# Padding TensorE's program: the fetch times of the search and the grain of its places

## The chip, the cores and the metric

The kernel runs on one core of a Trainium2 chip. The metric is the device time of one execution in microseconds; lower is better. Three runs of the kernel before gave 807.34 (the median), 804.82 and 808.4 us.

## The reference

Two blocks with residuals. The first is a recurrent attention over 64 segments of 32 tokens: eight memory rows stand ahead of each segment's tokens, and the eight memory rows that come out of a segment go into the next, so the segments form a chain. The second block is a pre-norm MLP (512 to 1792 to 512, tanh-gelu) on the result.

```python
for s in range(n_seg):                                  # 64 segments of 32 tokens
    h = jnp.concatenate([mem, xs], axis=1)              # 8 memory rows + 32 tokens, 512 wide
    q = jnp.einsum('btd,dhe->bhte', h, Wq)              # 32 heads of 128; k and v alike
    scores = jnp.where(mask, einsum(q, k) * scale, -1e9)
    o = jnp.einsum('bhqk,bhke->bhqe', softmax(scores), v)
    o = jnp.einsum('bhte,hed->btd', o, Wo)
    mem = o[:, :M, :].copy()                            # into the next segment
    outs.append(o[:, M:, :])
h = x + A(layernorm(x));  h2 = h + B(layernorm(h))
```

## The kernel before

All operations are recorded first. A scheduler (class `Sched`, lines 136 to 660) then sets the order on each engine, wires the semaphores and emits the program. On TensorE the order of a segment is written out by hand (`ORDERS`, line 39), as a list of parts; on the other engines a table of due times (`PLAN`, line 45) sets it. The parts of a segment are, in TensorE's order:

- Q0 and K0, in turns, and then Q1 and K1: the projections of the memory rows' part of `h` (`hT`) with Wq and Wk, in units of four 128x512 matmuls (lines 686 and 943);
- V0, SC0, V1, SC1, V1: the projection with Wv, in two halves, and between its units the scores' correction by the mask and the memory (SC0 and SC1, line 1119, sixteen matmuls each that wait for `BD` and `ZC`, which GpSimd makes);
- F: four filler units of work that is not on the chain, for the token blocks ahead or behind (lines 686, 943 and 1300). Two stand ahead of PV0, one ahead of SA, one behind it;
- PV0, PVA, PV1: the products of probabilities and values (lines 1150, 1154, 1222 and 1228), which wait for the values `VS` that ScalarE casts;
- WO: eight units of the output projection, 64 matmuls of 128x256 (line 1261). VectorE turns their result into the next segment's `hT` (`TT`, line 1273; `hT`, line 1267);
- SA: scores of 32 matmuls (line 1176), which cover the time until that `hT` is there.

So a segment ends when WO has gone through VectorE, and Q0 of the next waits for it.

**Fetches of the program.** TensorE's instructions come in blocks of 256 (`FETCH_N`; 16 KB, one transfer on the queue that the profile calls q8 instruction). The scheduler chooses where in the stream a block begins. It can add weight loads that nothing uses ("pads", line 941) to the units of the projections. A unit has at most `PADS` of them and a block at most `PAD_MAX`, counted in steps of `PAD_STEP`. A dynamic program (`pads`, line 494) goes over all places at which a block can begin, and adds up a cost for each pair of successive beginnings:

```python
wait = LATE.get("F2" if part == "F" and behind else part, 1.0) + ...      # line 516
c = c0 + sum(w * max(0.0, f + FETCH_TOOK + FETCH_IN + m - took) for m, w in FAR) + 1e-4 * p   # line 542
g = round(max(late[b], f + FETCH_TOOK + FETCH_REST - took), 1)            # line 543
```

Here `took` is the planned time between the two beginnings. `f` is the time from the entry of a block until the fetch of the next one starts; it is taken from the table `LATE` by the unit in which the block begins ("F2" is an F behind PVA). `FETCH_TOOK` is how long a fetch lasts, and `FETCH_IN` the time from its landing to the first instruction that can be used. What is left over is a stall of TensorE. Below, a place "enters" a part when the first instruction of a block lies in it.

Two other steps read the result: `windows` (line 392) puts the DMAs of SyncE's queue into the time behind a fetch, and `pauses` (line 371) gives up to three units behind a block's beginning a wait on earlier work of TensorE itself.

Of the kernel before, what the change touches and what calls it, by code (L numbers as in the profile page):

```python
# [21 lines left out]
DMA_SEMS, SOFT_SEMS = 100, 8  # L22
SORT = True
FETCH_N, FETCH_US = 256, 0.0
FETCH_AT, PADS, PAD_MAX, PAD_STEP = 65, 8, 104, 8
FAR = ((-0.1, 1.0), (0.2, 0.6), (0.5, 0.2))
FETCH_TOOK, FETCH_REST, FETCH_IN, LAST = 1.2, 2.45, 1.1, 1.5
LATE = dict(Q0=0.1, K0=0.1, Q1=-0.5, K1=-0.4, V0=2.0, SC0=2.0, SC1=1.6, V1=1.8, F=1.3, PV0=1.0, PVA=1.0, PV1=0.95, WO=0.4, F2=0.5, SA=0.5)
KEEP = True
WINDOWS, WIN_LO, WIN_HI, WIN_BEHIND = True, 1.0, -0.8, 0.4  # L30
PAUSES, PAUSE_IN, PAUSE_US = 3, 64, 0.5
# [108 lines left out]
class Sched:  # L140
# [353 lines left out]
    def pads(self):  # L494
# [17 lines left out]
        for i in range(lo, hi):  # L512
            o, n = pe[i], where[i + 1] - where[i]
            part = "" if o.tag is None else o.tag[1]
            behind = part == "PVA" or behind and part not in ("Q0", "K0")
            wait = LATE.get("F2" if part == "F" and behind else part, 1.0) + LAST * (o.tag is None or o.tag[0] == NS - 1)
            for k in range(n):
# [133 lines left out]
F = 1792  # L651
# [1122 lines left out]
```

## Time and profile before

| | |
|---|---|
| median of 3 runs | 807.34 us |
| profiled execution | 809.47 us, span 807.7 us, TensorE's mean granted clock 0.992 |
| TensorE matmul busy | 771.6 us, 96% of the span |
| VectorE, ScalarE, GpSimd busy | 588.0, 530.4, 312.0 us |
| instruction fetches | 156 packets of 16 KB |

The profiled execution is one run, 2.13 us above the median of the three. Its span is 1.77 us shorter than its time; that rest lies around the program. Groups of instructions are named by line, engine, operation and tiles; "PEld" is the weight load and "PE" the matmul. A row of the timeline gives a start, the duration of a run of equal instructions, their number, and in brackets the idle time ahead of them with what ended it ("issue" is time in which the engine waited for nothing that the profile shows).

### The profile page before, as it was taken

What the parts mean: (1) busy time and instruction counts of PE and PEld (TensorE: products, weight loads), DVE (VectorE), ACT (ScalarE), POOL (GpSimd) and SP (SyncE); (2) the same over time, 40 slices, a digit from 0 to 9 for tenths busy, and PEclk for the clock granted to TensorE, in tenths of its full rate; (3) what the DMA queues carried; (4) which work ended last, traced back from release to release, by engine and by line L of the source; (5) the groups of instructions that cost most, each with busy time, mean ns of one, the idle gap of its engine ahead of it and who ended that gap; (6) DMA issues with size and microseconds to landing.
All of it is one profiled execution on the core that took longest, in us unless ns stands there. A gap on an engine that the chain in (4) does not pass through costs nothing.

```text
span 807.7 us, 44856 instructions
## 1 busy us (share of the span) xinstructions
PE 771.6 (96%) x19564; PEld 423.2 (52%) x20093; DVE 588.0 (73%) x1865; ACT 530.4 (66%) x1380; POOL 312.0 (39%) x836
## 2 busy tenths in 40 slices
PE   3688999999999999999999999999999999899998
PEld 1345455555555555555655555556655554444443
DVE  3267888888888888888888888888897888723211
ACT  2446777777677777777767777767777777733342
POOL 3013223444443434344434444434443434267200
PEclk9979999999999999999999999999999999999999
DMA  9960000111101010101010101020112221255200
GB/s 338 393 189 12 2 23 18 27 33 27 33 20 41 18 42 18 43 15 47 14 47 9 51 6 47 11 50 4 50 30 66 53 59 40 75 140 167 73 27 26
DMA packets 65453, 48.11 MB, mean 60 GB/s; under 512 B 29028, under 2 KB 61676, under 8 KB 65260
## 3 DMA queue, kind: packets, MB, share of 16 engines
q1 hardware_dynamic: 64928, 44.98, 19.6%
q8 instruction: 156, 2.56, 1.3%
q14 instruction: 37, 0.30, 0.1%
q10 hardware_dynamic: 332, 0.27, 0.1%
HBM read 31.08 MB, written 8.13 MB: 49 GB/s over the span
## 4 chain that ended last, share of the span: by engine, by line
PE 91%; DVE 3%; DMA 2%; SPq 2%; ACT 1%; issue 1%; POOL 0%; DVEq 0%; POOLq 0%
PE high L943 33%; PE high L686 17%; PE quad L1261 15%; PE quad L1663 6%; PE high L1656 5%; PE high L1300 3%; DMA WQ<-in_A_Wq_dram 2%; PE quad L1119 2%; SPq L846 2%; PE quad L1176 2%; PE quad L1222 2%; PE high L1455 1%; PE high L1150 1%; PE quad L1150 1%; PE high L1261 1%
## 5 line engine op out<-in xcount | busy, mean ns | idle before, releaser
L943 PE MATMUL high<-WQ,hT 128*32 128x512 bf16 x1796 | 157.8, 381 | 3.1 <-DVE hT L1267 2.7
L1199 POOL TENSOR_TENSOR PA<-SA,rsa 128x256 bf16<-128x256 f32 x64 | 39.6, 619 | 237.1 <-DVE rsa L1191 139.3
L686 PE MATMUL high<-WK,hT 128*32 128x512 bf16 x1260 | 127.6, 379 | 0.1
L1261 PE MATMUL quad<-WO,OT 128*32 128x256 bf16 x4032 | 122.4, 273 | 0.2 <-issue 0.2
L943 PE MATMUL high<-WV,hT 128*32 128x512 bf16 x1528 | 116.4, 380 | 0.0
L962 ACT ACTIVATE kq<-high 128x512 bf16<-128x512 f32 x160 | 94.2, 598 | 27.2 <-PE high L943 24.4
L961 ACT CAST kq<-high 128x512 bf16<-128x512 f32 x159 | 92.6, 582 | 22.0 <-PE high L943 20.5
L1261 PEld LDWEIGHTS quad<-WO,OT 128*32 128x32 bf16 x4032 | 102.3, 97 | 6.1 <-issue 1.4
L1207 POOL COPY BD<-PTA 32x128 f32<-32x128 f32 x256 | 79.9, 312 | 16.8 <-DVE PTA L1203 0.6
L943 PEld LDWEIGHTS high<-WQ,hT 128*32 128x32 bf16 x1796 | 52.0, 95 | 61.3 <-issue 27.2
L984 DVE STREAM_TRANSPOSE KALL<-kq 128x256 f32<-128x256 f32 x160 | 69.5, 435 | 12.0 <-ACT kq L961 9.1
L961 ACT CAST VS<-high 128x512 bf16<-128x512 f32 x126 | 73.1, 580 | 0.0
L941 PEld LDWEIGHTS <-hT 128*32 128x32 bf16 x3064 | 49.8, 96 | 33.4 <-DVE hT L1267 6.3
L1273 DVE STREAM_TRANSPOSE TT<-quad 128x256 f32<-128x256 f32 x63 | 28.3, 449 | 50.7 <-PE quad L1261 50.6
L1659 ACT ACTIVATE WQ<-high,b1t 128x512 bf16<-128x512 f32 x42 | 28.9, 687 | 51.9 <-PE high L1656 51.9
L961 ACT CAST OT<-quad 128x128 bf16<-128x128 f32 (+1 forms) x128 | 47.8, 375 | 21.8 <-PE quad L1154 21.5
L1018 ACT COPY KALL<-KALL 128x128 f32<-128x128 f32 x62 | 18.4, 297 | 59.0 <-PE quad L1176 58.8
L984 DVE STREAM_TRANSPOSE QT<-kq 128x256 f32<-128x256 f32 x128 | 54.9, 429 | 1.4 <-ACT kq L962 1.2
L943 PE MATMUL high<-WK,hT 128*32 128x512 bf16 x788 | 55.3, 379 | 0.0
L1119 PEld LDWEIGHTS quad<-KALL,ZC 128*32 128x32 bf16 x2016 | 32.3, 96 | 42.3 <-POOL BD L1207 18.4
L686 PE MATMUL high<-WV,hT 128*32 128x512 bf16 x520 | 53.8, 382 | 0.0
L1313 POOL TENSOR_TENSOR opT<-TTB,TTS 32x64 bf16<-32x64 f32 x128 | 40.1, 313 | 34.9 <-DVE opT L1267 18.3
(184 smaller groups left out, 1620.3 us busy)
## 6 DMA issues: line engine op xcount, KB each, us to landing
WV<-in_A_Wv_dram SPq DMA_DIRECT2D x4, 1024.0 KB, 10.2
WK<-in_A_Wk_dram SPq DMA_DIRECT2D x4, 1024.0 KB, 17.9
WQ<-in_A_Wq_dram SPq DMA_DIRECT2D x4, 1024.0 KB, 20.2
WO<-in_A_Wo_dram SPq DMA_DIRECT2D x16, 256.0 KB, 7.6
v_last<-VSB SPq DMA_DIRECT2D x60, 64.0 KB, 2.2
VBD<-v_last SPq DMA_DIRECT2D x60, 64.0 KB, 2.6
h_mid<-xr SPq DMA_DIRECT2D x16, 128.0 KB, 2.2
WQ<-h_mid SPq DMA_DIRECT2D x4, 512.0 KB, 4.3
```

What stands on the lines that cost most here:

```text
L686: return e.add_instruction(mybir.InstMatmult(name="I-%d" % (4000000 + _kept[0]), engine=mybir.EngineType.PE, start_tensor_calc=start, stop ...
L941: e.ldweights(l, tile_position=(0, 32 * j))
L943: ins = e.matmul(o, l, m, start=(k == 0), stop=(k == DC - 1), tile_position=(0, 32 * j), skip_group_check=True)
L961: return {"act": (lambda e: e.copy(out, src), t_act(n, ps_)), "dve": (lambda e: e.tensor_copy(out, src), 0.155 + 1.0e-3 * n * fast)}
L962: return {"act": (lambda e: e.mul(out, src, scale_), t_act(n, ps_)), "dve": (lambda e: e.tensor_scalar(out, src, scale_, None, ALU.mult), ...
L984: S.op("dve", lambda e: e.transpose(out, src), reads=[("kq", i)], writes=[key], dur=t_dve(256) + 0.02)
L1119: ins = e.matmul(o[32 * j:32 * j + 32, :], zc_window(h), rhs, start=False, stop=(i == 3), tile_position=(0, 32 * j), skip_group_check=True)
L1207: S.narrow(S.op("pool", lambda e, j=j, rows=rows: e.tensor_copy(words(BD[rows, par, :, j, :, :]), words(PTA[rows, 0:4])), reads=["PTA"], w ...
L1261: ins = e.matmul(ps[bank][32 * j:32 * j + 32, 0:256], lhs(slot(h)), wo_cols(h, b), start=(k == 0), stop=(k == 15), tile_position=(0, 32 * ...
L1313: return e.tensor_tensor(o[32 * q:32 * q + 32, c:c + 2], x, y, ALU.add)
L1656: ins = e.matmul(ps[bank][:, 0:SBT], W1[:, cc, fc * P:(fc + 1) * P], hnT_of(k)[:, cc, :], start=(cc == 0), stop=(cc == DC - 1))
L1663: S.op("pe", lambda e: e.matmul(quad[:, t, :], gT_of(k, fc)[:, t * P:(t + 1) * P], W2[:, fc, :], start=(fc == 0), stop=(fc == FC - 1)), re ...
```

## The change

Three lines of constants change; no function does.

```diff
 FETCH_N, FETCH_US = 256, 0.0
-FETCH_AT, PADS, PAD_MAX, PAD_STEP = 65, 8, 104, 8
+FETCH_AT, PADS, PAD_MAX, PAD_STEP = 65, 12, 144, 4
 FAR = ((-0.1, 1.0), (0.2, 0.6), (0.5, 0.2))
-FETCH_TOOK, FETCH_REST, FETCH_IN, LAST = 1.2, 2.45, 1.1, 1.5
-LATE = dict(Q0=0.1, K0=0.1, Q1=-0.5, K1=-0.4, V0=2.0, SC0=2.0, SC1=1.6, V1=1.8, F=1.3, PV0=1.0, PVA=1.0, PV1=0.95, WO=0.4, F2=0.5, SA=0.5)
+FETCH_TOOK, FETCH_REST, FETCH_IN, LAST = 1.2, 2.45, 1.38, 1.5
+LATE = dict(Q0=0.4, K0=0.6, Q1=0.0, K1=1.25, V0=2.0, SC0=2.0, SC1=1.6, V1=1.85, F=1.55, PV0=1.1, PVA=1.1, PV1=1.05, WO=0.7, F2=0.9, SA=0.9)
```

The streams of VectorE (1,709 rows), ScalarE (1,173) and GpSimd (501) are row for row those of before. On SyncE's queue a few issues (`v_last`, `h_mid`, `xT`) trade places. TensorE's matmuls keep their order. What moves is the pads: 3,224 before (403 units with 8 each) and 3,252 now (254 units with 12, 17 with 8, 17 with 4). The number of blocks stays 156, so what changes is where they begin. Over the segments 1 to 63 the beginnings fall into these parts:

| part entered | WO | K1 | F | SA | Q1 | Q0 | PV1 | K0 | SC1 | PVA | V0, PV0 |
|---|---|---|---|---|---|---|---|---|---|---|---|
| before | 24 | 26 | 24 | 19 | 14 | 13 | 13 | 8 | 0 | 4 | 2 |
| now | 30 | 22 | 14 | 7 | 16 | 16 | 15 | 7 | 14 | 3 | 3 |

**At the start of segment 27, on TensorE.** `WQ,hT` is a unit of Q0 or Q1, `WK,hT` one of K0. Before:

```order
L686 MATMUL high<-WK,hT 32x512 x4
L943 MATMUL high<-WQ,hT 32x512 x4
L686 MATMUL high<-WK,hT 32x512 x4
L686 MATMUL high<-WQ,hT 32x512 x4
L943 MATMUL high<-WQ,hT 32x512 x12
```

Now, from the same rows (three of the four matmuls of each unit, with their pads, left out):

```order
L686 MATMUL high<-WK,hT 32x512
L941 LDWEIGHTS hT x3
...
L686 MATMUL high<-WQ,hT 32x512
L941 LDWEIGHTS hT x3
L943 MATMUL high<-WQ,hT 32x512
...
L941 LDWEIGHTS hT
L943 MATMUL high<-WQ,hT 32x512
```

Three unused loads now stand ahead of each matmul there (12 in a unit, some units have 4), where there were none. The block that begins in Q0 of this segment ends, with them, in SC1; before, a block that began in Q1 ended in PV1.

**From SC1 to the last WO unit of segment 27, on TensorE**, where a block now begins inside the first row below and the next one inside the WO row. The rows are the same before and now:

```order
L1119 MATMUL quad<-KALL,ZC 32x64 x16
L943 MATMUL high<-WV,hT 32x512 x8
L1300 MATMUL high<-WO,OTB 32x512 x16
L1150 MATMUL quad<-PTC,VS 128x2x8 x8
L1154 MATMUL quad<-PTC,VBD 128x64 x2
L1222 MATMUL quad<-BD,VS 128x2x32 x16
L1228 MATMUL quad<-BDL,VBD 128x8x8 x4
L1150 MATMUL high<-PTC,VS 128x2x8 x8
L1154 MATMUL high<-PTC,VBD 128x64 x2
L1261 MATMUL quad<-WO,OT 32x256 x64
```

Nothing in this stretch can take a pad, so its length in time is fixed. From SC1 (one of its last three instructions of 33) to the twelfth of the sixteen instructions of WO's last unit it is one block in six segments (11, 19, 27, 35, 43 and 51). In eight others (6, 14, 22, 30, 38, 46, 54 and 57) the block that begins in SC1 ends in the F unit ahead of SA, just behind WO.

## The prediction

> **What bounds the kernel now.** I read the page first, for the busy shares and the chain that ended last.
>
> ```profile
> PE 771.6 (96%) x19564; PEld 423.2 (52%) x20093; DVE 588.0 (73%) x1865; ACT 530.4 (66%) x1380; POOL 312.0 (39%) x836
> q8 instruction: 156, 2.56, 1.3%
> PE 91%; DVE 3%; DMA 2%; SPq 2%; ACT 1%; issue 1%; POOL 0%; DVEq 0%; POOLq 0%
> ```
>
> TensorE is the bound, and its matmuls keep their order. So the change can only win or lose time in which TensorE has nothing to do, or is slowed. The second row gives a mean fetch: 1.3% of 16 engines over 807.7 us, by 156, is 1.08 us.
>
> Then I read the period of a segment from VectorE's transposition of WO's result, which comes once a segment. The first row is its group with the first and last start; the others are single ones of the timeline (start, duration).
>
> ```profile
> L1273 DVE STREAM_TRANSPOSE TT<-quad x63: 411/450/452, 61.7 to 698.2; 128x256 f32<-128x256 f32 x63
> ...
> 307.58 0.45 DVE L1273 STREAM_TRANSPOSE TT<-quad 128x256 f32<-128x256 f32 x1 [1.22 <-PE quad L1261]
> 317.71 0.45 DVE L1273 STREAM_TRANSPOSE TT<-quad 128x256 f32<-128x256 f32 x1 [0.41 <-PE quad L1261]
> ...
> 410.02 0.45 DVE L1273 STREAM_TRANSPOSE TT<-quad 128x256 f32<-128x256 f32 x1 [0.91 <-PE quad L1261]
> 420.60 0.45 DVE L1273 STREAM_TRANSPOSE TT<-quad 128x256 f32<-128x256 f32 x1 [0.51 <-PE quad L1261]
> 430.69 0.45 DVE L1273 STREAM_TRANSPOSE TT<-quad 128x256 f32<-128x256 f32 x1 [1.22 <-PE quad L1261]
> ...
> 667.17 0.45 DVE L1273 STREAM_TRANSPOSE TT<-quad 128x256 f32<-128x256 f32 x1 [0.50 <-PE quad L1261]
> 698.19 0.45 DVE L1273 STREAM_TRANSPOSE TT<-quad 128x256 f32<-128x256 f32 x1 [1.24 <-PE quad L1261]
> ```
>
> 636.5 us over 62 periods is 10.266 us a segment. The best take 10.09 (420.60 to 430.69), others 10.58 (410.02 to 420.60). 62 times the difference of 0.176 is **10.9 us: all that better places can win.** The last three periods take 31.02 us, 0.75 over 30.27, though few pads lie there; I put 1.7 us of the 10.9 (0.7 to 3) to other causes. That leaves 9.2 for fetches.
>
> What such a stall is shows in the weight loads ahead of SA, in segment 35 and, without a stall, in segment 25.
>
> ```profile
> 406.07 0.77 PEld L1300 LDWEIGHTS high<-WO,OTB 128*32 128x32 bf16 x16
> 407.26 0.17 PEld L1150 LDWEIGHTS quad<-PTC,VS 64*128 64x128 bf16 x8 [0.42 <-ACT VS L961]
> 410.79 0.28 PEld L1176 LDWEIGHTS quad<-KALL,QT 128*32 128x32 bf16 x32 [0.89 <-issue]
> ```
>
> ```profile
> 303.66 0.11 PEld L943 LDWEIGHTS high<-WQ,hB 128*32 128x32 bf16 x4
> 304.85 0.17 PEld L1150 LDWEIGHTS quad<-PTC,VS 64*128 64x128 bf16 x8 [0.64 <-ACT VS L961]
> 307.57 0.51 PEld L1176 LDWEIGHTS quad<-KALL,QT 128*32 128x32 bf16 x32 [0.22 <-issue]
> ```
>
> In both, one block begins in the F units (406.1, 303.66) and the next in SA (410.79 and 307.8, inside the row that starts at 307.57). The DMA view of short windows tells when the next block was fetched. For 406.1 to 407.95 it has no row of that queue; for 407.95 to 409.35 it has the first row below. For 303.7 to 305.5 it has no packet at all (second row), and for 305.5 to 306.5 the third.
>
> ```profile
> q8 instruction: 1, 0.02, 5.9%
> DMA packets 0, 0.00 MB, mean 0 GB/s; under 512 B 0, under 2 KB 0, under 8 KB 0
> q8 instruction: 1, 0.02, 5.7%
> ```
>
> 5.9% of 16 engines over 1.4 us is a fetch of 1.32 us, so it started within 0.08 us of 407.95 and landed at 409.3. SA's first load came 1.46 to 1.52 us later. In segment 25 it took 0.91 us, started 1.84 to 1.93 us after the entry, and landed at 306.5, 1.3 us before SA went on. So a stall is: wait from entry to the fetch's start (1.85 from F), the fetch (1.08), landing to use (1.3 to 1.5), less the time between the two places.
>
> **The change part by part.**
>
> *The pads themselves: 0.* A unit with 12 pads issues 16 loads, one with 8 issues 12. Windows of one unit of Q0 or K0 each, in a padded stretch (the second number in brackets is of weight loads):
>
> ```profile
> 309.21:309.42 0.21, 0.21 (x8) 0.15 (x12) 0.21 (x2) 0.21 (x2) 0.00 (x0) 1.00 0.00 0
> 309.42:309.64 0.22, 0.22 (x9) 0.13 (x9) 0.22 (x2) 0.22 (x1) 0.00 (x0) 1.00 0.00 0
> 309.64:309.86 0.22, 0.22 (x10) 0.16 (x13) 0.22 (x2) 0.22 (x2) 0.00 (x0) 1.00 0.00 0
> ```
>
> From 9 loads to 13 the loads' busy time goes from 0.13 to 0.16 us, 8 ns a load, and a unit stays at 0.22. Four more make 0.19, still below; the four matmuls of the unit hide them. Without that cover they would cost 0.03 us in each of 254 units, 7.6 us in all; I take 0. *SyncE's DMAs that trade places: 0.* Of the page's issues these are the two that recur each segment, one behind the other:
>
> ```profile
> v_last<-VSB SPq DMA_DIRECT2D x60, 64.0 KB, 2.2
> VBD<-v_last SPq DMA_DIRECT2D x60, 64.0 KB, 2.6
> ```
>
> They take 4.8 us of a period of 10.27, so about 5 us of slack hides a shift; if one came late, PV0 or PVA would wait for `VBD`, at most the shift of one fetch window, some 1 us in few segments.
>
> *The stalls that go.* By the table of places, F to SA comes 7 times instead of 18 or 19. The Q0 and K0 entries that followed 3.0 to 3.5 us behind the one before (about 21) now follow after 3.5 us or more but for two; PV1 entered from K1 (3) and the second F of a segment from its first (3) are gone. So some 46 short pairs carry the 9.2 us, 0.2 us each. The 7 that remain run from F's first unit to the eighth instruction of SA, a shape like segment 25's: 10.13 us from 307.58 to 317.71, 0.04 over the floor. I take 0.06 each, **0.4** (bounds 0 and 7 x 0.2 = 1.4). The two short Q0 and K0 pairs (3.2 and 3.3 us) keep 0.25 each, **0.5**. For fetches that happen to last 1.3 or 1.4 us where the pair has little to spare (WO, K1) I take **1.0** (0 to 2.0).
>
> *The stalls that come.* Fourteen blocks now begin in SC1, which none did before, and the table's 1.6 us for it is unchanged. Segment 27, loads:
>
> ```profile
> 323.56 0.21 PEld L1119 LDWEIGHTS quad<-KALL,ZC 128*32 128x32 bf16 x16 [0.31 <-POOL BD L1207]
> 323.69 0.14 PEld L943 LDWEIGHTS high<-WV,hT 128*32 128x32 bf16 x8
> ...
> 325.12 0.17 PEld L1150 LDWEIGHTS quad<-PTC,VS 64*128 64x128 bf16 x8 [0.42 <-ACT VS L961]
> ...
> 325.90 1.65 PEld L1261 LDWEIGHTS quad<-WO,OT 128*32 128x32 bf16 x64
> 327.55 0.22 PEld L1300 LDWEIGHTS high<-WO,OTB 128*32 128x32 bf16 x8
> ```
>
> The last load of SC1 starts at 323.67 (0.21 less a load's 0.097 behind 323.56). The 62nd of WO's loads starts at 325.90 + 61 x 0.0247 = 327.41, and the F unit ahead of SA at 327.55. So six pairs have 3.74 us (SC1 to WO) and eight 3.88 (SC1 to F). F to SA has 3.91 (303.66 to 307.57 in segment 25) and costs 0.2 with F's 1.85, so fetch and landing together count as 3.91 + 0.2 - 1.85 = 2.3 (less than 1.08 + 1.3, since loads run a little ahead of their matmuls). With L for the wait after an entry in SC1, the cost is 6 (L + 2.3 - 3.74) + 8 (L + 2.3 - 3.88), as far as the brackets are positive.
>
> L isn't in the trace. Three rows bound it. The shortest of such waits is SA's: segment 25's block begins at 307.8, and the view shows no fetch until 308.85 and one of 0.96 us that lands by 309.9, so 1.1. The longest is F's. It could be an event that sets it: in the segments 25 and 35 the fetch starts 0.65 to 0.75 us behind the first load of PV0 (304.85, 407.26), which waited for ScalarE. In SC1's case that is 325.12 + 0.7 - 323.67 = 2.15. But segment 51 speaks against it:
>
> ```profile
> 570.62 0.76 PEld L1300 LDWEIGHTS high<-WO,OTB 128*32 128x32 bf16 x16
> 571.80 0.17 PEld L1150 LDWEIGHTS quad<-PTC,VS 64*128 64x128 bf16 x8 [0.42 <-ACT VS L961]
> ...
> q8 instruction: 1, 0.02, 5.8%
> ```
>
> The last row is of 572.0 to 573.2; there is none from 570.6 to 572.0. It lasted 1.11 us, so it began by 572.09, less than 0.3 us behind PV0. In this segment PV0 stands 29 instructions behind the beginning of the block, in the segments 25 and 35 it is 23 and 29. What could hold the fetch instead is a wait that `pauses` puts on the F units themselves; in SC1's blocks such a unit stands 0.45 us behind the entry, and from there F's fetches began 0.8 (segment 51) to 1.45 us later. That gives L = 1.25 to 1.9: nothing at the low end, 6 x 0.46 + 8 x 0.32 = 5.3 at 1.9. I take about half of it, **2.8** (bounds 0, and at 2.15 us 6 x 0.71 + 8 x 0.57 = 8.8).
>
> *The sum.* 1.7 + 0.4 + 0.5 + 1.0 + 2.8 = 6.4 us of stall stay of 10.9: 4.5 less. The profiled execution would come to 805.0. It lies 2.1 us above the median of the runs; the median goes to **802.8**.
>
> [...]
>
> **The rivals.**
>
> *Entries in SC1 wait 1.1 to 1.4 us, as in SA.* For it: SC1 is of SA's kind, short matmuls that follow quickly. Then the last term is 0: 3.6 of 10.9 stay, 7.3 less, 800.0. It holds up to L = 1.44. Chance 0.27.
>
> *Entries in SC1 wait for PV0's values, and the stall moves from SA to WO and F.* Place: the last unit of WO (or F) behind SC1. For it: segments 25 and 35. Against it: segment 51. At L = 2.15 it is 3.6 + 8.8 = 12.4, 808.8. The point from which the change loses is where the term reaches the other 7.3: 14 L - 21.3 = 7.3, so L = 2.04. A stall in WO also makes the next `hT` late, and Q0 waits for that; at L = 2.4, which a fetch that starts 0.25 us later still would give, the term is 12.3 and the time 812.3. Chance 0.19, of which 0.07 at 2.35 or more.
>
> *The search doesn't do what it says: the stalls aren't fetches' but move with other things.* The 10.09 and 10.58 would stay: 807.3. Against it: the stall of 410.79 follows a landing, and no semaphore. Chance 0.09.
>
> *Sixteen loads don't fit a unit.* 7.6 us by the bound above on top of 802.8, 810.4. Against it: 0.19 of 0.22 us. Chance 0.03.
>
> **How the numbers follow.** The forecast (L of 1.4 to 2.0) has 0.42, with 800 to 807 as its own range, and 802.8 as its point. I call 0.5%, 4.0 us, what a measurement can tell: faster is below 803.3, slower above 811.4. Faster: the first rival's 0.27 and half of the forecast (0.22), 0.49. Slower: 0.07 of the second rival, half of the last (0.02) and 0.02 for what I don't see, 0.11. The rest, 0.40, is no change. The range leaves out the best tenth (all bounds low: 0.7 + 0 + 0.3 stay, 797.4) and the worst: 798.8 to 809.8.
>
> **What would show it.** In the trace after: the period of a segment at 10.09 to 10.15 in the segments without SC1 entries, and in the 14 with them the start of the fetch behind SC1, 1.25 to 1.9 us after the entry. Idle time with "issue" ahead of SA should fall from 11.6 us, and come, if L is large, ahead of line 1300 or 943 behind WO, or inside WO. Units with 16 loads should stay at 0.22. The forecast is wrong if periods of 10.09 become longer (pads that cost), or if the SC1 segments take 10.5 or more.
>
> ```profile
> PEld quad L1176 <- issue: 11.6, 45, 0.9
> ```

## The result, and the profile after

The change made the kernel slower: 813.24 us (median of 5 runs, 810.59 to 815.02) against 807.34 us (median of 5, 804.82 to 808.4). The ratio is 1.0076, with a 95% interval of 1.0055 to 1.0097. The prediction was 802.8, faster. The profiled execution took 815.02 us, with a span of 813.3.

The page after, in the rows shown of before:

```profile
PE 774.5 (95%) x19573; PEld 420.6 (52%) x20121; DVE 587.2 (72%) x1865; ACT 530.5 (65%) x1380; POOL 310.7 (38%) x836
q8 instruction: 156, 2.56, 1.4%
PE 90%; DVE 2%; DMA 2%; SPq 2%; issue 1%; ACT 1%; POOL 0%; DVEq 0%; POOLq 0%
```

The shares hardly move; the period of a segment does. Here is VectorE's transposition again, the group and some single ones:

```profile
L1273 DVE STREAM_TRANSPOSE TT<-quad x63: 433/450/451, 60.9 to 703.7; 128x256 f32<-128x256 f32 x63
...
400.05 0.45 DVE L1273 STREAM_TRANSPOSE TT<-quad 128x256 f32<-128x256 f32 x1 [0.41 <-PE quad L1261]
411.37 0.45 DVE L1273 STREAM_TRANSPOSE TT<-quad 128x256 f32<-128x256 f32 x1 [1.98 <-PE quad L1261]
...
441.75 0.45 DVE L1273 STREAM_TRANSPOSE TT<-quad 128x256 f32<-128x256 f32 x1 [0.41 <-PE quad L1261]
452.86 0.45 DVE L1273 STREAM_TRANSPOSE TT<-quad 128x256 f32<-128x256 f32 x1 [1.04 <-PE quad L1261]
...
681.38 0.45 DVE L1273 STREAM_TRANSPOSE TT<-quad 128x256 f32<-128x256 f32 x1 [1.22 <-PE quad L1261]
693.34 0.45 DVE L1273 STREAM_TRANSPOSE TT<-quad 128x256 f32<-128x256 f32 x1 [1.14 <-PE quad L1261]
```

642.8 us over 62 periods is 10.37 us. Over a floor of 10.09 that is 17.2 us of stall, where before had 10.9. The span grew by 5.6. In segment 35, whose block goes from SC1 to WO, the period is 11.32 us. Behind segment 38, whose block goes from SC1 to F, it is 11.11. Added up over the 14 segments with a block from SC1, the excess over 10.09 is 11.2 us: 5.0 in the periods of the six that end in WO, 6.2 in the periods behind the eight that end in F. The period that ends at 693.34 has 1.87 more. In it (segment 62) a block begins in V0, a place that the prediction passed over.

Where the time is lost shows in segment 35's weight loads on the timeline:

```profile
405.90 0.21 PEld L1119 LDWEIGHTS quad<-KALL,ZC 128*32 128x32 bf16 x16 [0.31 <-POOL BD L1207]
406.17 0.13 PEld L943 LDWEIGHTS high<-WV,hT 128*32 128x32 bf16 x8
406.39 0.76 PEld L1300 LDWEIGHTS high<-WO,OTB 128*32 128x32 bf16 x16
407.58 0.17 PEld L1150 LDWEIGHTS quad<-PTC,VS 64*128 64x128 bf16 x8 [0.42 <-ACT VS L961]
...
408.31 1.64 PEld L1261 LDWEIGHTS quad<-WO,OT 128*32 128x32 bf16 x62
411.04 0.10 PEld L1261 LDWEIGHTS quad<-WO,OT 128*32 128x32 bf16 x2 [1.09 <-issue]
```

TensorE stops ahead of the last two of WO's 64 loads, for 1.09 us, exactly at the beginning of the next block. The DMA view of the stretch from 406.2 to 408.5 has no row of the instruction queue; that of 408.5 to 409.6 has this:

```profile
q8 instruction: 1, 0.02, 5.0%
```

5.0% of 16 engines over 1.1 us is a fetch of 0.88 us, so it began at 408.5 to 408.7. That is 2.3 to 2.5 us behind the block's first instruction (406.17), and 0.9 to 1.1 us behind the first load of PV0 (407.58). In segment 38 it is the same with F in WO's place. The next fetch began 2.0 to 2.2 us after the entry at 437.60. From 437.7 to 439.6 the DMA view has no packet of any queue, so no transfer of the kernel's own stood in its way; one fetch of 1.23 us lies between 439.6 and 441.0:

```profile
437.60 0.14 PEld L943 LDWEIGHTS high<-WV,hT 128*32 128x32 bf16 x8
...
439.03 0.17 PEld L1150 LDWEIGHTS quad<-PTC,VS 64*128 64x128 bf16 x8 [0.64 <-ACT VS L961]
...
441.41 0.10 PEld L943 LDWEIGHTS high<-WV,hB 128*32 128x32 bf16 x2
442.40 0.10 PEld L943 LDWEIGHTS high<-WV,hB 128*32 128x32 bf16 x2 [0.89 <-issue]
```

From here on, *the wait of a block* means the time from its first instruction to the start of the next fetch. Over the 14 SC1 blocks of the change it is 1.05 and 1.39 us in two (segments 11 and 22) and 1.87 to 2.46 in twelve, 2.01 in the mean. In the twelve the fetch starts 0.46 to 1.04 us behind PV0's first load; in the two it starts ahead of it. A least distance between two fetches doesn't hold them: they start 3.6 to 4.9 us behind the landing of the fetch before, and elsewhere in the same trace a fetch starts 2.35 us behind it.

### The profile page after: what moved, and what is told of

Same layout as the page of the kernel before. It is cut to its first block, busy times and chain, and to the rows that moved or that the text cites. A ratio compares the mean times of both kernels' runs of the same rounds, so it can differ in the third digit from the quotient of the medians.

```text
span 813.3 us, 44890 instructions
## 1 busy us (share of the span) xinstructions
PE 774.5 (95%) x19573; PEld 420.6 (52%) x20121; DVE 587.2 (72%) x1865; ACT 530.5 (65%) x1380; POOL 310.7 (38%) x836
## 4 chain that ended last, share of the span: by engine, by line
PE 90%; DVE 2%; DMA 2%; SPq 2%; issue 1%; ACT 1%; POOL 0%; DVEq 0%; POOLq 0%
PE high L943 33%; PE high L686 17%; PE quad L1261 15%; PE quad L1663 6%; PE high L1656 5%; PE high L1300 3%; DMA WQ<-in_A_Wq_dram 2%; PE quad L1119 2%; SPq L846 2%; PE quad L1176 2%; PE quad L1222 2%; PE high L1455 1%; PE high L1150 1%; PE quad L1150 1%; PE high L1261 1%
## 5 line engine op out<-in xcount | busy, mean ns | idle before, releaser
L1261 PEld LDWEIGHTS quad<-WO,OT 128*32 128x32 bf16 x4032 | 102.4, 97 | 10.9 <-issue 5.7
L941 PEld LDWEIGHTS <-hT 128*32 128x32 bf16 x3084 | 42.3, 95 | 22.4 <-DVE hT L1267 7.0
```

Source lines behind the costliest of these rows:

```text
L941: e.ldweights(l, tile_position=(0, 32 * j))
L1261: ins = e.matmul(ps[bank][32 * j:32 * j + 32, 0:256], lhs(slot(h)), wo_cols(h, b), start=(k == 0), stop=(k == 15), tile_position=(0, 32 * ...
```

## The experiments

Ratios are to the kernel before on the same chip, with 95% intervals. The medians of the kernel before were 806.0, 804.9 and 807.0 us in the three groups of runs.

### First group: which part of the change, and what holds the fetch

**The first line alone.** `LATE` and `FETCH_IN` are those of before.

```diff
-FETCH_AT, PADS, PAD_MAX, PAD_STEP = 65, 8, 104, 8
+FETCH_AT, PADS, PAD_MAX, PAD_STEP = 65, 12, 144, 4
```

> The change's first line alone (12 pads in a unit, 144 in a block, steps of 4) with the old times. No block begins in SC1 then; 22 go from F to SA, 21 begin in Q0. If the loss comes from the blocks that begin in SC1 (theory), this is near the kernel before: 805 to 810 us. If more pads in a unit are what costs (rival), it is as slow as the change, 812 to 814.

Measured: 808.47 us, ratio 1.0032 (1.0016 to 1.0047). Near before, as the theory has it, though a little slower. 23 blocks begin in SA then, and the idle time with "issue" ahead of SA's loads (the waits of the weight loads: us in total, times, longest) is as large as before's 11.6 (most of it is the 0.22 us that SA's loads have in a segment without a stall too, as in segment 25):

```profile
PEld quad L1176 <- issue: 11.6, 46, 0.8
```

**The two other lines alone.** The grain is that of before (8, 104, 8).

> The new times with the old grain (8 pads, 104, steps of 8). 17 blocks begin in SC1, 11 of them end in WO and 6 in F. Theory (a block that begins in SC1 gets the next fetch only 2.1 us later, because the wait of PV0 stands in between): slower than before, 811 to 816. Rival (the pads cost): as before or faster, 803 to 808.

Measured: 815.08 us, ratio 1.0119 (1.0104 to 1.0134). So the new times carry the loss; the first line alone brought 0.3%. The new table makes F's, K1's and the others' waits longer and leaves SC1 at 1.6; that is what drives the search into SC1. 14 of the 17 SC1 blocks there waited 1.81 to 2.40 us, three 0.97 to 1.03.

**The whole change with 2.15 for SC1.**

```diff
-LATE = dict(..., SC1=1.6, V1=1.85, F=1.55, ...)
+LATE = dict(..., SC1=2.15, V1=1.85, F=1.55, ...)
```

> The whole change with 2.15 us for SC1 in the table in place of 1.6. No block begins in SC1 then; 14 go from F to SA, 6 from F to F. Theory: the 8 to 10 us of the SC1 pairs go and some 4 us come back in F's pairs, 803 to 807. Rival (the rest of the change is what costs): 811 or more.

Measured: 804.02 us, ratio 0.9982 (0.9970 to 0.9995). One number of the table, which the search needs and which no trace of before could give, turns 1.0076 into 0.9982.

**Six self-waits in place of three.** This and the runs behind it ask why SC1 blocks wait so long. A self-wait is one of the waits on TensorE's own earlier work that `pauses` adds behind a block's beginning; `PAUSES` is how many there can be, and `PAUSE_US` how far ahead of its unit the plan has each of them released.

```diff
-PAUSES, PAUSE_IN, PAUSE_US = 3, 64, 0.5
+PAUSES, PAUSE_IN, PAUSE_US = 6, 64, 0.5
```

> The change with up to six self-waits behind a block's beginning in place of three; the places stay. In an SC1 block the fourth goes to the second F unit, the last one ahead of PV0. Theory (the sequencer asks for the next block only while it issues; it runs ahead to PV0's wait and stands there): the fourth self-wait lets it issue later, the wait for the fetch in SC1 blocks falls from 2.1 to 1.0 to 1.5 us, and the time to 803 to 808. Rival (the fetch is tied to PV0's release itself, or to a count of instructions): it stays at 2.0 to 2.4 us, 811 to 815.

Measured: 808.83 us, ratio 1.0026 (1.0010 to 1.0042), just above the range; but the SC1 blocks split as the edit does. The six that end in WO have short F units ahead of PV0, and the last self-wait there is released 0.43 us after the entry, by the scheduler's plan. Five of these waited 1.09 to 1.39 us and one 1.76. The eight that end in F have long F units, and the last release is at 0.22 us. Six of these stayed at 1.99 to 2.10, and two (22 and 57) were at 1.03 and 1.09. Segment 35, loads and the DMA view of 403.6 to 405.4 (there is no such row from 402.5 to 403.6):

```profile
402.46 0.13 PEld L943 LDWEIGHTS high<-WV,hT 128*32 128x32 bf16 x8
...
403.87 0.16 PEld L1150 LDWEIGHTS quad<-PTC,VS 64*128 64x128 bf16 x8 [0.42 <-ACT VS L961]
...
q8 instruction: 1, 0.02, 5.8%
```

5.8% of 16 engines over 1.8 us is 1.67 us, so the fetch began at 403.6 to 403.73, 0.14 us or more *ahead* of PV0's first load. In the change it began some 1 us behind it. The stall in WO is gone. TensorE's group of WO's matmuls in the change and then in this run (us of idle time ahead of them at the end):

```profile
L1261 PE MATMUL quad<-WO,OT 128*32 128x256 bf16 x4032 | 123.8, 273 | 3.8 <-issue 3.7
```

```profile
L1261 PE MATMUL quad<-WO,OT 128*32 128x256 bf16 x4032 | 122.7, 273 | 0.5 <-issue 0.5
```

### Second group: number of self-waits or time of their release

**Six self-waits, released 0.25 us ahead of their unit.**

```diff
-PAUSES, PAUSE_IN, PAUSE_US = 3, 64, 0.5
+PAUSES, PAUSE_IN, PAUSE_US = 6, 64, 0.25
```

> The change with up to six self-waits that are released 0.25 us ahead of their unit in place of 0.5. In the run with six at 0.5 us, the SC1 blocks whose last self-wait is released 0.43 us after the entry (by the plan) got their fetch after 1.1 to 1.4 us, those with 0.22 us after 2.0. Now it is 0.44 us in the latter too. Theory (a release later than some 0.3 us after the entry is what counts): the eight SC1 blocks that end in F come down to 1.0 to 1.4 us as well, 803 to 806 us. Rival (the number of self-waits counts, or the distance to PV0): they stay at 2.0, 807 to 811.

Measured: 805.01 us, ratio 1.0002 (0.9984 to 1.0020), inside the theory's range. The eight SC1 blocks that end in F, with as many self-waits as in the run before and only their release moved to 0.44 us, came down to 1.04 to 1.14 (five) and 1.56 to 1.59 (three), and none of them stalls in F any more. Segment 38:

```profile
433.44 0.14 PEld L943 LDWEIGHTS high<-WV,hT 128*32 128x32 bf16 x8
...
434.86 0.17 PEld L1150 LDWEIGHTS quad<-PTC,VS 64*128 64x128 bf16 x8 [0.63 <-ACT VS L961]
...
437.25 0.11 PEld L943 LDWEIGHTS high<-WV,hB 128*32 128x32 bf16 x4
```

437.25 follows WO without the 0.89 us that stood at this place in the change. The six that end in WO went the other way, though their release moved to 0.65 us: 1.14 and 1.15 in two, 1.64 to 1.96 in four. So the time of the last release isn't all of it.

**The same, with 2.15 for SC1.**

> The change with 2.15 us for SC1 (no block begins there) and six self-waits at 0.25 us. Theory: F's blocks have two long units ahead of PV0, whose last self-wait is released at 0.2 us or earlier, so they gain little: 801 to 805. Rival (later self-waits hold TensorE up): 806 or more.

Measured: 803.63 us, ratio 0.9998 (0.9978 to 1.0018). In the range in us, but no better by the ratio than three self-waits at 0.5 us with the same places (0.9982). Where no block begins in SC1, more self-waits show no gain.

**No self-waits.**

```diff
-PAUSES, PAUSE_IN, PAUSE_US = 3, 64, 0.5
+PAUSES, PAUSE_IN, PAUSE_US = 0, 64, 0.5
```

> The change without any self-wait; the places stay. Theory: the two of the 14 SC1 blocks that got their fetch early (1.0 and 1.4 us) join the others at 2.0 to 2.5, and no other place gains: 813 to 818. Rival (the self-waits themselves cost, or play no part): 811 or less, or the same 12 late and 2 early.

Measured: 831.13 us, ratio 1.0323 (1.0291 to 1.0354), far above the range. All 14 SC1 blocks waited 1.87 to 2.58 us, as the theory said. What it had not said is K1: of its 22 blocks, 20 went from 1.3 to 2.1 us to 2.5 to 2.96, and one (segment 3) from a fetch that began ahead of its entry to 2.95. The blocks behind them, which begin in WO, stalled for it.

```profile
L1261 PE MATMUL quad<-WO,OT 128*32 128x256 bf16 x4032 | 129.4, 273 | 17.1 <-issue 17.1
```

It is much the same at another place, though not with the next wait. Behind a K1 block stand the waits of V0 and SC0 first, and then that of SC1. In all 21 blocks the fetch starts 0.87 to 1.19 us behind SC1's first load, and 2.2 us or more behind SC0's, which comes 0.1 to 0.7 us after the entry. So a wait that ends early doesn't by itself bring the fetch. In segment 25 the block begins at 308.59, there is no packet of any queue until 311.1, and one fetch of 1.28 us from there to 312.5 (last row; the first is SC0's, the second SC1's):

```profile
308.90 0.28 PEld L1119 LDWEIGHTS quad<-KALL,ZC 128*32 128x32 bf16 x16 [0.43 <-DVE KALL L984]
...
310.18 0.21 PEld L1119 LDWEIGHTS quad<-KALL,ZC 128*32 128x32 bf16 x16 [0.30 <-POOL BD L1207]
...
313.78 0.45 PEld L1261 LDWEIGHTS quad<-WO,OT 128*32 128x32 bf16 x20 [0.96 <-issue]
...
q8 instruction: 1, 0.02, 5.7%
```

**The kernel before with six self-waits at 0.25 us.**

> The kernel before with six self-waits at 0.25 us; it has no block that begins in SC1. A control for what the self-waits do by themselves. Theory: within 2 us of before, 804 to 808. Rival (more and later self-waits help or hurt everywhere): 802 or less, or 810 or more.

Measured: 804.53 us, ratio 1.0002 (0.9982 to 1.0022). The control holds: more and later self-waits show no gain by themselves.

### Third group: few but late self-waits, and a table read anew

**At most three self-waits, none on a unit that starts within 0.4 us of the block's beginning, released 0.25 us ahead.**

```diff
-                if not o.waits and 0 <= j < i:
+                if not o.waits and 0 <= j < i and o.start >= pe[first].start + 0.4:
```

> The change with at most three self-waits again, but only on units that start 0.4 us or more behind the block's first one, released 0.25 us ahead. An SC1 block that ends in F then has two (released 0.0 and 0.44 us after the entry) in place of three early ones. Theory (the time of the last release counts): SC1's fetches start after 1.0 to 1.6 us in most of the 14, 803 to 807 us. Rival (the number of self-waits counts): 2.0 us as with three early ones, 811 to 814.

Measured: 806.37 us, ratio 1.0001 (0.9980 to 1.0021). 13 of the 14 SC1 blocks waited 0.96 to 1.40 us, one 2.0. Two or three late self-waits do in SC1's blocks what three early ones don't, so it is not their number there.

**The same, with 2.15 for SC1.**

> The same late self-waits with 2.15 us for SC1, so that no block begins there. Theory: the 14 pairs from F to SA remain as they are (F has only long units ahead of PV0), 802 to 805 us. Rival (K1's blocks need the early self-waits): K1's fetch comes after 2.5 us as without any, 810 to 825.

Measured: 808.91 us, ratio 1.0039 (1.0012 to 1.0066). Neither was right. K1's blocks, which the rival named, stayed at 1.3 to 2.3 us. But F's blocks, 26 of them here, lost their early self-waits and got fetches as late as 2.3 to 2.5 us, and stalls came ahead of the F units of line 1300. This goes against the theory of the release: in the segments 15, 23, 31 and 47 an F block with three self-waits, released 0.5 us ahead of units that start 0.20 to 0.63 us behind the entry, got its fetch after 0.80 to 0.96 us. Here it has one, released 0.25 us ahead of a unit at 0.67, and the fetch came after 1.92 to 2.49 us. The waits of its loads, first with three self-waits at 0.5 us and 2.15 for SC1, then here:

```profile
PEld high L1300 <- issue: 0.7, 2, 0.4
```

```profile
PEld high L1300 <- issue: 3.7, 6, 0.9
```

**Six self-waits at 0.25 us, and the table read anew from that run.**

```diff
+FETCH_TOOK, FETCH_REST, FETCH_IN, LAST = 1.1, 2.45, 1.4, 1.5
+LATE = dict(Q0=0.85, K0=1.1, Q1=-0.1, K1=1.5, V0=2.0, SC0=2.0, SC1=1.4, V1=1.85, F=1.6, PV0=0.95, PVA=1.3, PV1=1.0, WO=1.0, F2=0.85, SA=0.95)
```

> Six self-waits at 0.25 us, and the table read anew from that run (SC1 1.4, F 1.6, K1 1.5, SA 0.95 and so on; fetch 1.1, landing to use 1.4). The search then takes 22 places in SC1, 14 of them to WO. Theory: with fetches 1.0 to 1.6 us after SC1 few stalls are left, 799 to 804 us. Rival (part of the SC1 blocks still wait for PV0, 1.7 to 2.0 us): 804 to 809.

Measured: 805.11 us, ratio 0.9983 (0.9969 to 0.9998): in the rival's range in us. Yet the reason was the theory's: of the 22 SC1 blocks, 19 waited 1.02 to 1.18 us and three 1.52 to 1.73, and WO hardly waits:

```profile
L1261 PE MATMUL quad<-WO,OT 128*32 128x256 bf16 x4032 | 122.5, 273 | 0.2
L1273 DVE STREAM_TRANSPOSE TT<-quad x63: 411/449/452, 60.5 to 694.8; 128x256 f32<-128x256 f32 x63
```

62 periods take 634.3 us (second row), 8.7 over the floor. In the run with 2.15 for SC1 and three self-waits it is 8.5:

```profile
L1273 DVE STREAM_TRANSPOSE TT<-quad x63: 432/450/451, 60.7 to 694.8; 128x256 f32<-128x256 f32 x63
```

So the two best versions keep nearly the same rest, by quite different places. What that rest consists of was not taken apart.

Those two, at 0.9982 and 0.9983, beat the kernel before by about 0.2%, and the change by 0.9%.

The SC1 blocks over all runs, by the wait from their first instruction to the next fetch:

| self-waits of the run | SC1 blocks | up to 1.45 us | 1.5 to 1.8 | over 1.8 | ratio |
|---|---|---|---|---|---|
| none | 14 | 0 | 0 | 14 | 1.0323 |
| three at 0.5 us (the change) | 14 | 2 | 0 | 12 | 1.0076 |
| three at 0.5 us, new times alone | 17 | 3 | 0 | 14 | 1.0119 |
| six at 0.5 us | 14 | 7 | 1 | 6 | 1.0026 |
| six at 0.25 us | 14 | 7 | 5 | 2 | 1.0002 |
| at most three, late | 14 | 13 | 0 | 1 | 1.0001 |
| six at 0.25 us, table read anew | 22 | 19 | 3 | 0 | 0.9983 |

## Why the prediction was wrong

**The step that failed** is the term of the stalls that come: L, the wait of an SC1 block, was put at 1.25 to 1.9 us and its cost at 2.8. L measured 2.01 in the mean, 2.15 without the two early ones, and the cost was 11.2 by the periods. It was the second rival, with a chance of 0.19, that came true: place, price at L = 2.15 (8.8 us) and sign were its own.

- *The evidence that I set against the rival was read wrongly.* In segment 51 the fetch starts less than 0.3 us behind PV0, and I concluded that PV0's wait doesn't hold it and that a self-wait on an F unit does. But of the 21 F blocks of before that have PV0 ahead of them, three (31, 51 and 59) get the fetch 0.11 to 0.28 us behind PV0's first load, and 18 get it 0.49 to 1.06 us behind it. The lag of 0.65 to 0.75 in the segments 25 and 35 was the rule, and the trace of before showed it. In the change, too, two of 14 get the fetch ahead of PV0. I let one exception change the estimate for all.
- *What the runs put in its place:* in 12 of the 14 SC1 blocks the fetch comes behind PV0's wait, at 2.15 us in the mean; with at most three later self-waits ahead of PV0, 13 of the 14 get it at 0.96 to 1.40 us. The reading that I take from it is that the request for the next block is made while TensorE's sequencer issues, and not while it stands at a wait: a sequencer that reaches a wait for another engine too early would make the request only when that wait is over. It is an interpretation; no view shows the request or how far the sequencer is ahead of the instructions that run. An SC1 block has PV0's wait 42 to 49 instructions behind its beginning, and the reading needs the sequencer to stand at it before the block has got that far; that is not shown. What the runs show is the times: with six self-waits at 0.5 us, where the last one ahead of PV0 is released 0.43 us after the entry, five of six blocks get the fetch at 1.09 to 1.39 us (in segment 35 at least 0.14 us ahead of PV0's first load) and one at 1.76; where it is released at 0.22 us, two of eight get it at 1.03 and 1.09 and six at 1.99 to 2.10. Two sets of blocks don't fit the reading: K1's without self-waits, where SC0's wait ends 0.1 to 0.7 us after the entry and the fetch starts 2.2 us or more behind it, and the F blocks in which three early self-waits brought the fetch after 0.80 to 0.96 us and a later one after 1.92 to 2.49.
- *The size of a stall was nearly right, with the right L.* For the five WO stalls, L + 2.3 - 3.74 gives 0.65, 0.43, 0.97, 1.02 and 0.69 us; the idle time of WO's loads in the trace is 0.51, 0.54, 1.09, 1.09 and 0.81. Summed over all 14 with their own L, the formula gives 7.5 us. The other 3.7 of the 11.2 is what I left out: behind a stall in F, SA's loads take 0.62 us in place of 0.41, and the stretch from Q0 to SC0 of the next segment 3.77 in place of 3.54, seven times (1.6); TensorE loses up to 0.2 us between SC1 and PV0 where a block begins in SC1 (0.8 in the six that end in WO); the rest is small stalls of other kinds in the same periods. With the 1.9 us of segment 62 this leaves 4.1 of the 17.2 us for everything else, where the other terms of the prediction came to 3.6.
- *The stalls that go* did go: the idle time with "issue" ahead of SA fell from 11.6 to 9.2 (the row below). That sign says little, though: both hold 0.22 us for each of 45 and 38 times, which segment 25 has without a stall, and beyond it are 1.7 us before and 0.8 now. The F to SA pairs, six (the seventh SA block follows PV0), cost 1.0 and not 0.4, within the bound of 1.4: three of them fell on long fetches, 1.28 to 1.38 us, and cost 0.22 to 0.30 each, by the periods behind them. That term was taken from the likeness to segment 25, one block with a fetch of 0.91 us.

```profile
PEld quad L1176 <- issue: 9.2, 38, 0.6
```

- *The pads* cost nothing, as put. Units with 12 pads take 0.215 to 0.216 us, as those with none do; that ends the fourth rival. (The first line alone was 0.3% slower, with 23 blocks in SA; I did not take that apart further.) The third (the stalls aren't fetches) falls with the run without self-waits: 18 us more than the change from waits alone, and 17.1 us of idle time ahead of WO's matmuls in place of 3.7, where blocks begin.
- *The first rival* (L as in SA, 1.1 to 1.4) failed with L. What SA has and SC1 lacks is probably a next wait that is over early; no run tests it. Behind an SA block it is Q0's for `hT`. Q0's first load comes 0.4 to 0.9 us behind the entry, PV0's 1.4 us behind that of SC1 (406.17 to 407.58).
- *What I left out altogether* is V0 in segment 62. Its block waited 3.35 us, and WO's loads then stood idle for 1.36 us; the period is 1.87 us over the floor. The waits of SC1 and PV0 stand in between, but that they hold the fetch isn't shown: the block that begins in V0 in segment 2 has them too, and waited 1.05 us.
- *The chances:* slower had 0.11, of which 0.07 for L at 2.35 or more. With L at 2.01 the result still passed 0.5%, because of the 3.7 us of follow-ups and the 1.9 of segment 62, none of which was in any term.

What stays open: why some blocks with a late enough release still wait (six at 0.25 us: 7 of 14 over 1.5 us, with releases at 0.44 and 0.65 us), why in F's blocks several early self-waits did more than one later, and what exactly must have happened before the sequencer asks. No run took PV0's wait away, so that PV0's wait holds the twelve fetches rests on adding, moving and removing the self-waits ahead of it, and not on its own removal.

## What to carry to other kernels

A table of delays "by place" that is fitted to a trace holds only for the places that the trace contains. A search over such a table will go where the entry is a guess; put a pessimistic value there first, as 2.15 for SC1 did here (0.9982 instead of 1.0076).

Where instruction fetches bound an engine, look at the semaphore waits behind the beginning of a block. In 12 of 14 SC1 blocks of the change the next fetch started only behind PV0's wait; a wait on the engine's own earlier work, released 0.43 or 0.44 us after the block begins by the plan, brought the fetch from some 2 us to 1.04 to 1.39 in ten of the 14. It is no rule for every place: in four F blocks one such wait, released 0.42 us after the entry by the plan, left the fetch at 1.92 to 2.49 us.

One block that behaves otherwise is no argument against a pattern that most others show; ask first what was different in it.

## What was not expected of the hardware

- Without self-waits the change goes from 1.0076 to 1.0323 of the kernel before, though one would expect a wait to cost time and not to save it. K1's blocks then wait 2.5 to 2.96 us for the next fetch in place of 1.3 to 2.1, and WO's matmuls have 17.1 us of idle time ahead of them.
- The waits of the SC1 blocks come in groups in the two runs of the change's places with six self-waits: 1.03 to 1.20 us thirteen times, 1.39 once, 1.56 to 1.76 six times, 1.86 to 2.10 eight times. No run tells why.
- From the landing of a fetch to the first instruction of its block TensorE took 1.19 to 1.53 us wherever it stood waiting for it in the change (once 1.59), whether the instruction was a load of SA, F or WO.
